# Spreading GpSimd's weight sums and splits over three blocks of a feature group in a two-layer attention and SwiGLU kernel

## The chip, the cores and the metric

The kernel runs on one core of one Trainium2 chip. A core has five engines that run side by side and wait for each other through semaphores: TensorE (PE in the profile; PEld is its weight load), VectorE (DVE), ScalarE (ACT), GpSimd (POOL) and SyncE (SP), which here issues nearly all DMAs. Each engine works through its own list of instructions in order. The metric is the device time of one execution in microseconds (us); lower is better. A time is given as the median of several runs.

## The reference

Four layers in a row on x of 2048 rows and 448 columns, all in float32: attention, feed-forward, attention, feed-forward, with the same attention weights and the same feed-forward weights both times.

```python
x = x + A(layernorm(x)); x = x + B(layernorm(x)); x = x + A(layernorm(x)); x = x + B(layernorm(x))
# A: 16 heads of 28 columns for q, one shared head for k and v
scores = einsum("bhqd,bkd->bhqk", q, k) * 28 ** -0.5;  p = softmax(scores)
o = einsum("bhqk,bkd->bhqd", p, v);  A = o @ wo
# B: gate and up 448 -> 1792, down 1792 -> 448
B = (silu(x @ w_gate) * (x @ w_up)) @ w_down
```

## The kernel before

Matrix products run in fp32r, a rounded float32. To keep precision, each operand is split in a high part (rounded to fp32r) and a low part (what is left), and a product is the sum of three matmuls. `split` does this on GpSimd with two instructions: `tensor_scalar` for the high part (L139) and `tensor_tensor` with a subtraction for the low part (L140).

The change is in the feed-forward stage, which the kernel runs twice (layers 0 and 1; in the profiled execution from about 562 to 943 us and from about 1562 to 2005 us). The 2048 rows are held as four chunks of 512. The 1792 features are 14 blocks of 128, numbered `fc`; two of them make a feature group, so there are seven groups, numbered `gi`.

Groups 0 and 6 are "old" groups. They go by `unit(gi, c, n)`: one chunk, one feature block, with gate, up and down computed straight. Groups 1 to 5 are "mixed" groups and go by `blocked(gi)`: four blocks j0 to j3, each for a pair of chunks (p = 0 or 1) and one of the group's two features A and B, in the order (0, A), (0, B), (1, A), (1, B). There, on the first two 128-row slices of the contraction, seven products take the place of eight. This needs sums and differences of weights (the tiles S, made by `sums` on GpSimd: four `tensor_tensor` of 128 columns at L800 to L803, then one split of 512 columns) and of inputs (the tiles T, made by `mix` at L787 to L792: 18 instructions for a pair of chunks; the pair p = 0 on GpSimd into the tiles `keys`, the pair p = 1 on VectorE into the tiles `mixed`).

The weights of a feature come in by `columns` (gate and up: four DMAs into the tile `wr`, two of them of 192 KB and two of 64 KB) and `loaded` (the same and a DMA of 224 KB into `wdr`). There is one buffer of `wr` and one of `wdr`, so a load waits until the readers of the one before are done. `parted` then splits them in six pieces (four of `wgh`/`wgl`, two of `wdh`/`wdl`), 12 GpSimd instructions. Three sets of split weights are kept.

The order of work is written out by hand. In a mixed block it is the string `ORDER`: names in order of issue, where a trailing "-" means the step of the block before and "--" of the one before that. The marks w1, w2, x2, x3 in it are places where `run` slips in further jobs. A step such as `Ec2`/`Ep2` first has ScalarE copy a finished down product out of a PSUM bank into a `stage` buffer (L879; there are two) and then GpSimd add it to the residual `xres` (L886). `between` (L344) is a tiny ScalarE copy from a bank that keeps two halves of TensorE work in order; TensorE waits for it. In the units the same takes are L995 (ScalarE), L996 (GpSimd) and L992 (VectorE, the other half of the adds).

At the stage's begin `rest` issues, in this order on GpSimd: the two instructions of the layer norm of chunk 3 (`rstd`, L237 and L238), the sums of feature 2, and the first six of the 18 mix steps. The other twelve follow four at a time, one lot in each of the next three units (`self.more`). VectorE's 18 mix steps (`self.extra`) begin in the unit of chunk 3: six in each of two units, then three in each of the blocks j0 and j1 of group 1, at x2 and x3. `turned` on chunk 3 transposes its normalized rows on TensorE (L287) after four small GpSimd copies (L248).

In the mixed groups GpSimd's weight work before the change is: at w1 of j0 the split of the second feature of the group; at w1 of j1 the sums and the whole split of the next group's first feature; at w1 of j3 the sums of the next group's second feature.

Of the kernel before, what the change touches and what calls it, by code (L numbers as in the profile page):

```python
# [17 lines left out]
D = 448  # L18
# [8 lines left out]
FG = 2  # L27
# [25 lines left out]
def forward(  # L53
# [72 lines left out]
    def rows3(dst, src):  # L126
        n = src.shape[1]
        nc.sync.dma_start(dst[:, 0:3], src[0:384, :].rearrange("(k p) n -> p k n", p=P))
        nc.sync.dma_start(dst[:, 3], src[384:448, :][None].to_broadcast([2, 64, n]))
# [8 lines left out]
    def split(hi, lo, raw):  # L138
        nc.gpsimd.tensor_scalar(hi, raw, 1.0, 0.0, ALU.mult, ALU.add)  # L139
        nc.gpsimd.tensor_tensor(lo, raw, hi, ALU.subtract)  # L140
# [16 lines left out]
    def columns(fc):  # L157
        fs = slice(P * fc, P * fc + P)
        r = wpool.tile([P, 4, 2, P], F32, name="wr")
        for b, src in enumerate((w_gate, w_up)):  # L160
            rows3(r[:, :, b, :], src[:, fs])
        return r

    def loaded(fc):
        r = columns(fc)
        rd = wpool.tile([P, D], F32, name="wdr")
        nc.sync.dma_start(rd, w_down[P * fc : P * fc + P, :])
        return r, rd

    def weights(fc):  # L170
        return parted(*loaded(fc))

    def parted(r, rd):
        h = wpool.tile([P, 4, 2, P], F32R, name="wgh", bufs=FG + 1)
        l = wpool.tile([P, 4, 2, P], F32R, name="wgl", bufs=FG + 1)
        dh = wpool.tile([P, D], F32R, name="wdh", bufs=FG + 1)
        dl = wpool.tile([P, D], F32R, name="wdl", bufs=FG + 1)
        for k in range(4):
            split(h[:, k], l[:, k], r[:, k])
        for ns in (slice(0, 224), slice(224, D)):  # L180
            split(dh[:, ns], dl[:, ns], rd[:, ns])
        return h, l, dh, dl

    def load_wqkv(pool, first):

# [162 lines left out]
    class Attention:  # L348
# [106 lines left out]
        def fetch(self, ms):  # L455

            r = wpool.tile([P, 2, 512], F32R, tag="wgl", name="wrq", bufs=FG + 1).bitcast(F32)
            two = wpool.tile([P, 2, 512], F32R, tag="wgh", name="q2", bufs=FG + 1)
            for z, m in enumerate(ms):
                nc.sync.dma_start(r[0:112, z, :], self.qd[0][112 * m : 112 * m + 112, :])  # L460
                self.hi[m] = two[0:112, z, :]
            nc.gpsimd.tensor_copy(two[0:112], r[0:112])
# [309 lines left out]
    class FeedForward:  # L772
# [22 lines left out]
        def sums(self, fc, r):  # L795

            raw = self.apart
            m = [raw[:, P * i : P * i + P] for i in range(4)]
            tt = nc.gpsimd.tensor_tensor
            tt(m[0], r[:, 0, 1, :], r[:, 1, 1, :], ALU.add)  # L800
            tt(m[2], r[:, 0, 0, :], r[:, 0, 1, :], ALU.subtract)
            tt(m[1], m[0], r[:, 0, 0, :], ALU.subtract)
            tt(m[3], r[:, 1, 0, :], m[1], ALU.subtract)  # L803
            split(*self.S[fc % 3], raw)
# [106 lines left out]
        def blocked(self, gi):  # L911

            A, B = groups[gi]
            if not self.blocks:
                one, two, *adds = self.pend
                self.pend = []
                self.blocks.append({"E1": one, "E2": two, "Ea0": adds[0], "Ec2": lambda: [f() for f in adds[1:]]})
                self.tmp = pers.tile([P, 4, 512], F32, name="xn")
            last = gi == mixed[-1]

            def fetch(fc):
                self.raw = loaded(fc)

            def part(fc):
                self.W[fc] = parted(*self.raw)

            def sums(fc):
                if fc // FG in mixed:
                    self.sums(fc, self.raw[0])

            jobs = [
                {"w1": [lambda: part(B)] if gi > mixed[0] else [], "w2": [lambda: fetch(A + 2)]},
                {"w1": [lambda: sums(A + 2), lambda: part(A + 2)], "w2": [lambda: fetch(A + 3)]},
                {},
                {"w1": [lambda: sums(A + 3)]},
            ]
            for j, (p, fc) in enumerate((p, fc) for p in range(2) for fc in (A, B)):
                for n, k in (("x2", 1), ("x3", 2)):
                    jobs[j][n] = [self.extra.pop(0) for _ in range(min(k, len(self.extra)))]
                self.blocks.append(self.block(p, fc))  # L940
                self.run(jobs[j])
            if last:
                o = self.blocks[-1]
                self.blocks.append({})
                ends = [[o.pop(e + k) for k in e_.split()] for e, e_ in (("E", "1 2 a0 a1 a2 a3"), ("F", "1 2 a0 a1 a2 a3"))]
                fences = [o.pop("fE"), o.pop("fF")]
                for k in ("Ec2", "Ec3", "Ep2", "Ep3"):
                    del o[k]
                self.run({})
                part(A + 3)  # L950
                self.pend, self.late = (
                    [lambda f=f, g=g: (f[0](), g()), f[1], f[2], lambda f=f: [f_() for f_ in f[3:]]] for f, g in zip(ends, fences)
                )
# [97 lines left out]
        def unit(self, gi, c, n):  # L1051
            fs = groups[gi]
            fc = fs[n]
# [50 lines left out]
            self.pend = self.down(fs, fc, d, hh, hl)  # L1104
            if n == len(fs) - 1:
                self.pend += self.accumulate(gi, c, d)
            for fs_, k in ((self.more, 4), (self.extra, 6)):
                for _ in range(min(k, len(fs_))):
                    fs_.pop(0)()
            if c == NC - 1 and mixed and not fc:  # L1110

                def load():
                    r, rd = loaded(FG + 1)
                    self.sums(FG + 1, r)
                    self.W[FG + 1] = parted(r, rd)

                self.pend.append(load)
            elif c == NC - 1 and not mixed and fc + FG + 1 < NF:
                self.pend.append(lambda: self.W.__setitem__(fc + FG + 1, weights(fc + FG + 1)))

# [41 lines left out]
        def rest(self, xb):  # L1162
# [15 lines left out]
                f()  # L1178
            self.soon.append([1, lambda: [f() for f in third[5:]]])
            if mixed:  # L1180
                self.sums(FG, columns(FG))
                self.more = self.mix(0, nc.gpsimd, self.apart, lambda o, i: nc.gpsimd.tensor_scalar(o, i, 1.0, 0.0, ALU.mult, ALU.add))
                for f in self.more[:6]:
                    f()
                del self.more[:6]
# [64 lines left out]
    for c in range(1, NC):  # L1250
        fs, got = norm_steps(c)
        n = 4 * c - 4
# [38 lines left out]
```

## Time and profile before

| | |
|---|---|
| time, median of 3 runs | 2005.31 us (2001.29 to 2008.09) |
| profiled execution, own time | 2007.16 us |
| its span, first to last instruction | 2005.4 us |
| mean granted TensorE clock | 0.992 |
| busy: TensorE / VectorE / ScalarE / GpSimd | 98% / 53% / 68% / 40% |

A row of the timeline gives the start in us from the span's start, the duration in us, the engine, the line of the kernel, the operation, the tiles written and read ("out<-in"), shapes, how many instructions were merged into the row (x), and in brackets the engine's idle time just before and what ended it. A row of the windows gives the stretch, its length, the busy time of each engine with the number of instructions, the granted TensorE clock (1.00 is full speed), the DMA engines' busy share and the GB/s. A row of the waits gives in total us, how often, and the longest.

### The profile page before, as it was taken

The page shows a single profiled execution, that of the slowest core. Times are in us where ns is not written, and L with a number is a line of the kernel's source. Part 1 is how long each engine was busy: PE and PEld are TensorE (multiplying, and loading weights), DVE is VectorE, ACT ScalarE, POOL GpSimd, SP SyncE. Part 2 cuts the span into 40 slices and gives each one's busy share as a digit, 9 for nine tenths or more (in the row PEclk, how much of TensorE's full clock was granted, in tenths as well). Part 3 has the DMA queues.
Part 4 walks back from the last instruction along what each step waited for, and adds up shares of the span by engine and source line. Part 5 has one row for each costly group of instructions (what it writes and reads, how often), then busy time and mean ns, then how long its engine had stood idle before and what let it go on. Part 6 is the DMA issues. An engine that isn't in the chain of part 4 may idle for free. (4 is left out here: it accounts for less than half of the span.)

```text
span 2005.4 us, 45589 instructions
## 1 busy us (share of the span) xinstructions
PE 1965.1 (98%) x18267; PEld 1334.2 (67%) x18267; DVE 1067.9 (53%) x1777; ACT 1357.2 (68%) x2409; POOL 803.7 (40%) x1024
## 2 busy tenths in 40 slices
PE   9999999999998999999999999999999989999998
PEld 7544545445467999999884444454454779999997
DVE  7444543545436666665654335445454467666653
ACT  4899898998953444444349989989989334444432
POOL 4212211133219667765341221212241285767740
PEclk9999999999999999999999999999999999999999
DMA  5111110211110111000131011102111100111102
GB/s 164 52 29 30 30 46 12 54 35 47 52 28 17 30 32 32 21 28 26 51 106 37 27 30 31 43 13 61 48 49 34 37 16 16 32 32 31 30 3 75
DMA packets 95511, 78.63 MB, mean 39 GB/s; under 512 B 23582, under 2 KB 78494, under 8 KB 95294
## 3 DMA queue, kind: packets, MB, share of 16 engines
q1 hardware_dynamic: 95006, 75.21, 13.3%
q8 instruction: 144, 2.36, 0.5%
q14 instruction: 73, 0.60, 0.1%
q10 hardware_dynamic: 288, 0.46, 0.1%
HBM read 56.11 MB, written 18.74 MB: 37 GB/s over the span
## 5 line engine op out<-in xcount | busy, mean ns | idle before, releaser
L661 PE MATMUL bank<-pt,vsb 128*32 128x512 f32 x4096 | 493.3, 598 | 0.3
L620 PE MATMUL bank<-qstack,keys 32*128 32x512 f32 x1536 | 484.7, 425 | 0.0
L620 PE MATMUL three<-qstack,keys 32*128 32x512 f32 x4608 | 460.3, 425 | 1.5 <-DVE vt L554 1.2
L620 PEld LDWEIGHTS three<-qstack,keys 32*128 32x128 f32 x4608 | 254.1, 182 | 295.3 <-ACT pt L633 181.1
L627 ACT ACTIVATE pt<-three 128x1536 f32<-128x1536 f32 x256 | 372.3, 1454 | 0.8 <-PE bank L661 0.5
L633 ACT ACTIVATE pt<-three 128x1536 f32<-128x1536 f32 x256 | 372.1, 1453 | 0.0
L337 PE MATMUL bank<-xh,wgh 64*128 64x512 f32 x1248 | 359.4, 395 | 5.3 <-ACT sg L860 3.9
L337 PE MATMUL bank<-wdh,h 64*128 64x448 f32 x1776 | 344.3, 368 | 1.6 <-DVE xres L884 0.9
L629 DVE COPY raw<-bank 128x512 f32<-128x512 f32 x256 | 177.6, 694 | 226.4 <-PE bank L620 223.6
L337 PE MATMUL bank<-xh,wgl 64*128 64x512 f32 x924 | 283.3, 393 | 0.0
L671 DVE TENSOR_TENSOR o<-bank,o 128x512 f32<-128x512 f32 x224 | 155.0, 692 | 240.7 <-PE bank L661 236.0
L344 ACT COPY seen<-bank 128x1 f32<-128x1 f32 x820 | 105.1, 162 | 252.1 <-PE bank L337 178.4
L700 POOL TENSOR_TENSOR o<-o 128x512 f32<-128x512 f32 x32 | 41.2, 1286 | 583.9 <-DMA o<-rd 529.0
L661 PEld LDWEIGHTS bank<-pt,vsb 128*32 128x32 f32 x4096 | 107.1, 109 | 249.8 <-issue 152.6
L337 PEld LDWEIGHTS bank<-wdh,h 64*128 64x128 f32 x1776 | 261.0, 187 | 12.6 <-DVE xres L884 2.5
L886 POOL TENSOR_TENSOR xres<-stage,xres 128x448 f32<-128x448 f32 x152 | 190.2, 1267 | 177.0 <-ACT stage L879 177.0
L337 PE MATMUL bank<-xl,wgh 64*128 64x512 f32 x816 | 247.1, 394 | 0.0
L620 PEld LDWEIGHTS bank<-qstack,keys 32*128 32x128 f32 x1536 | 243.3, 183 | 0.8 <-DVE o L671 0.6
L337 PE MATMUL bank<-wdl,h 64*128 64x448 f32 x888 | 229.5, 371 | 0.0
L851 DVE TENSOR_TENSOR xn<-bank,xn 128x512 f32<-128x512 f32 x240 | 158.0, 686 | 131.9 <-PE bank L337 85.9
L337 PEld LDWEIGHTS bank<-xh,wgh 64*128 64x128 f32 x1248 | 201.6, 186 | 15.8 <-issue 3.5
L632 ACT ACTIVATE pt<-bank 128x512 f32<-128x512 f32 x256 | 151.5, 592 | 59.7 <-PE bank L620 59.6
(200 smaller groups left out, 3243.2 us busy)
## 6 DMA issues: line engine op xcount, KB each, us to landing
o<-rd SPq DMA_DIRECT2D x32, 256.0 KB
qraw<-qd SPq DMA_DIRECT2D x128, 56.0 KB
qd<-stage SPq DMA_DIRECT2D x30, 224.0 KB
xt<-xn SPq DMA_DIRECT2D x28, 224.0 KB
wdr<-in_B_w_down_dram SPq DMA_DIRECT2D x28, 224.0 KB
wr<-in_B_w_gate_dram SPq DMA_DIRECT2D x30, 192.0 KB
wr<-in_B_w_up_dram SPq DMA_DIRECT2D x30, 192.0 KB
xn<-xt SPq DMA_DIRECT2D x7, 768.0 KB
```

Of the source, the lines that this page charges most:

```text
L337: nc.tensor.matmul(po, a, b, start=start, stop=stop, skip_group_check=True)
L344: nc.scalar.copy(seen[:, i : i + 1], po[:, 0:1])
L620: nc.tensor.matmul(three[:, j, :] if j < 3 else one, k[js, kp, ks], q[js, part, :], start=(z == 0), stop=(z == 2), tile_position=(32 * j, 0),)
L627: nc.scalar.activation(pt, three, AF.Exp, scale=SCALE)
L629: nc.vector.tensor_copy(raw, one)
L632: nc.scalar.activation(pt1, one, AF.Exp, scale=SCALE)
L633: nc.scalar.activation(pt, three, AF.Exp, scale=SCALE)
L661: nc.tensor.matmul(po[32 * j : 32 * j + 32, :], vsb[:, n % NT, :], pts[n][j], start=(n == 2 * d), stop=(n > 2 * d), skip_group_check=True,)
L671: nc.vector.tensor_tensor(acc, in_turn(po), acc, ALU.add)
L700: nc.gpsimd.tensor_tensor(rb, oraw, rb, ALU.mult)
L851: plus = lambda out, po, r: tt(by_tile(out), in_turn(po), by_tile(r), ALU.add)
L886: nc.gpsimd.tensor_tensor(r, h[e, t], r, ALU.add)
```

## The change

There are four edits.

- In the mixed groups the split of the next group's first feature (12 instructions at w1 of j1) is cut in two: three of the six pieces at w2 of j1 and the other three at w1 of j2. The sums stay at w1 of j1. The load of the feature after that moves from w2 of j1 to w2 of j2, and its sums from w1 of j3 to w2 of j3.
- At the stage's begin the sums of features 2 and 3 are both made in `rest`, ahead of the mix steps. For feature 3 this is a `columns` load of its own, four more DMAs in each layer, 512 KB. The job that made the sums of feature 3 at the end of group 0 now only loads and splits that feature's weights.
- VectorE's mix steps in the two last units of group 0 are four in each instead of six.
- In the first two mixed blocks they are two at x2 and three at x3 instead of one and two.

```diff
     def weights(fc):
-        return parted(*loaded(fc))
+        tiles, steps = parted(*loaded(fc))
+        for f in steps:
+            f()
+        return tiles
...
-        for k in range(4):
-            split(h[:, k], l[:, k], r[:, k])
-        for ns in (slice(0, 224), slice(224, D)):
-            split(dh[:, ns], dl[:, ns], rd[:, ns])
-        return h, l, dh, dl
+        steps = [lambda k=k: split(h[:, k], l[:, k], r[:, k]) for k in range(4)]
+        steps += [lambda ns=ns: split(dh[:, ns], dl[:, ns], rd[:, ns]) for ns in (slice(0, 224), slice(224, D))]
+        return (h, l, dh, dl), steps
...
-            def part(fc):
-                self.W[fc] = parted(*self.raw)
+            def part(fc, z=None):
+                if not z:
+                    self.W[fc], self.steps = parted(*self.raw)
+                for f in self.steps[3:] if z else self.steps[: 6 if z is None else 3]:
+                    f()
...
                 {"w1": [lambda: part(B)] if gi > mixed[0] else [], "w2": [lambda: fetch(A + 2)]},
-                {"w1": [lambda: sums(A + 2), lambda: part(A + 2)], "w2": [lambda: fetch(A + 3)]},
-                {},
-                {"w1": [lambda: sums(A + 3)]},
+                {"w1": [lambda: sums(A + 2)], "w2": [lambda: part(A + 2, 0)]},
+                {"w1": [lambda: part(A + 2, 1)], "w2": [lambda: fetch(A + 3)]},
+                {"w2": [lambda: sums(A + 3)]},
             ]
             for j, (p, fc) in enumerate((p, fc) for p in range(2) for fc in (A, B)):
-                for n, k in (("x2", 1), ("x3", 2)):
+                for n, k in (("x2", 2), ("x3", 3)):
...
-            for fs_, k in ((self.more, 4), (self.extra, 6)):
+            for fs_, k in ((self.more, 4), (self.extra, 4)):
...
             if c == NC - 1 and mixed and not fc:
-
-                def load():
-                    r, rd = loaded(FG + 1)
-                    self.sums(FG + 1, r)
-                    self.W[FG + 1] = parted(r, rd)
-
-                self.pend.append(load)
+                self.pend.append(lambda: self.W.__setitem__(FG + 1, weights(FG + 1)))
...
             if mixed:
-                self.sums(FG, columns(FG))
+                for fc in (FG, FG + 1):
+                    self.sums(fc, columns(fc))
```

## The prediction

> **What bounds the kernel now.** I read the page's head and chain first, then TensorE's waits, then the timeline around each wait, then windows for the granted clock.
>
> ```profile
> span 2005.4 us, 45589 instructions
> PE 43%; POOL 3%; DVE 1%; ACT 1%; issue 1%; POOLq 0%; ACTq 0%; DVEq 0%
> ```
>
> ```profile
> PE bank L337 <- ACT seen L344: 12.5, 8, 2.6
> PE bank L337 <- DVE xn L851: 8.1, 3, 4.1
> ```
>
> TensorE sets the time, and the chain leaves it only for short stretches, above all on GpSimd (3%). Only there can this change win or lose anything. The largest wait of TensorE is for ScalarE's `seen` copies in mixed blocks: 12.5 us in 8 waits, six of about 2 us. The first and the last of the six:
>
> ```profile
> 736.22 0.51 PE L337 MATMUL bank<-mixed,qstack 64*128 64x512 f32 x1 [1.92 <-ACT seen L344]
> ...
> 1850.40 0.49 PE L337 MATMUL bank<-mixed,kdiag 64*128 64x512 f32 x1 [2.62 <-ACT seen L344]
> ```
>
> All six stand at the end of block j1 in groups 2, 3 and 4 of both layers. One of them, engine by engine:
>
> ```profile
> 1715.87 0.46 POOL L800 TENSOR_TENSOR apart<-wr 128x128 f32<-128x128 f32 x1
> 1720.08 0.42 POOL L139 TENSOR_SCALAR wgh<-wr 128x256 fp32r<-128x256 f32 x1
> ...
> 1728.02 4.47 POOL L886 TENSOR_TENSOR xres<-stage,xres 128x448 f32<-128x448 f32 x4
> ```
>
> ```profile
> 1718.90 1.15 ACT L879 COPY stage<-bank 128x448 f32<-128x448 f32 x2 [0.47 <-PE bank L337]
> ...
> 1729.20 0.53 ACT L879 COPY stage<-bank 128x448 f32<-128x448 f32 x1 [3.26 <-POOL xres L886]
> ```
>
> ```profile
> 1729.84 0.79 PE L337 MATMUL bank<-mixed,qstack 64*128 64x512 f32 x1 [1.93 <-ACT seen L344]
> ```
>
> GpSimd runs the sums (4.2 us, 1715.87 to 1720.08) and the whole split (7.9 us, to 1728.02) in one go. Behind them wait the two adds of the E step, whose stage buffers ScalarE filled from 1718.90. ScalarE's next take needs one of these buffers, idles 3.26 us, and its `seen` copies stand behind it, so TensorE idles 1.93 us. The wait then costs a second time:
>
> ```profile
> 1684.00:1698.00 14.00, 14.00 (x129) 13.85 (x127) 10.10 (x15) 6.85 (x26) 8.53 (x10) 1.00 0.00 1
> ...
> 1726.20:1743.20 17.00, 15.07 (x121) 14.63 (x120) 8.31 (x14) 6.26 (x25) 8.49 (x9) 0.90 0.16 46
> 1743.20:1758.00 14.80, 14.80 (x137) 14.70 (x136) 9.90 (x16) 7.58 (x27) 9.07 (x10) 1.00 0.00 1
> ```
>
> ```profile
> 736.60:740.00 3.40, 3.40 (x19) 3.35 (x18) 1.33 (x3) 1.70 (x4) 2.24 (x3) 0.50 0.08 25
> ...
> 1791.30:1794.70 3.40, 3.40 (x21) 3.40 (x19) 2.58 (x4) 1.18 (x6) 1.09 (x1) 0.50 0.02 6
> ```
>
> An undisturbed block takes 14.0 us; the two after the wait take 17.0 and 14.8, 3.8 us too long for an idle of 1.93. The rest is the clock: in 3.4 us after the wait it is 0.50. That is so after four of the six waits (the rows are the first and the last of the four); each such stretch loses half of itself, 1.7 us.
>
> **The change part by part.** *Cutting the split.* After the change GpSimd does in j1 the sums, then the E adds, then half a split, and the other half in j2. In the rows above the E adds would start at 1720.1 instead of 1728.0, and four adds took 4.47, so two are done at about 1722.4; half a split follows until about 1726.3, just when the F take comes; its add is late by less than 1 us and nothing waits for it. The other half at w1 of j2 holds up E adds by at most 4 us, as the sums now do in j1. Sums at w2 instead of w1 of j3 come behind the E adds and hold up none of them; their result is read a group later, and nothing else is queued before the next F take. I count nothing for them, 1 us if that cover is short. The moved load (five DMAs, issued a block later on SyncE, with nothing queued behind it there) has a block of 14 us until the sums read it. So all six waits go. Idle about 12.1 us (12.5 less two short waits), clock 4 x 1.7 = 6.8, and about 0.2 us each that the 3.8 us shows above 1.93 + 1.7: 20 us gained. Lower end 12, if only the idle comes back.
>
> *Sums of feature 3 at the stage's begin.* This is what speaks against the change. The rows in order, layer 1, then two other loads into the same tile `wr`:
>
> ```profile
> 1593.28 0.46 POOL L800 TENSOR_TENSOR apart<-wr 128x128 f32<-128x128 f32 x1
> ...
> 1595.14 0.46 POOL L803 TENSOR_TENSOR apart<-wr,apart 128x128 f32<-128x128 f32 x1
> ...
> 1597.77 1.28 POOL L787 TENSOR_TENSOR apart<-xh 128x512 f32<-128x512 f32 x1
> ...
> 1605.57 2.58 POOL L996 TENSOR_TENSOR xres<-stage,xres 128x448 f32<-128x448 f32 x2
> ...
> 1613.11 0.76 POOL L248 COPY xn<-xn 128x64 f32<-128x64 f32 x4
> ```
>
> ```profile
> 1595.63 0.37 SPq L128 DMA_DIRECT2D wr<-in_B_w_gate_dram  x1
> ```
>
> ```profile
> 1608.29 0.96 ACT L995 COPY stage<-bank 128x448 f32<-128x448 f32 x2
> ```
>
> ```profile
> 1613.40 0.85 PE L287 MATMUL bank<-ident,xn 128*128 128x128 f32 x4 [0.45 <-POOL xn L248]
> ```
>
> ```profile
> 957.39 0.38 SPq L128 DMA_DIRECT2D wr<-in_A_wq_dram  x1
> ```
>
> ```profile
> 963.04 0.94 POOL L139 TENSOR_SCALAR wh<-wr 128x896 fp32r<-128x896 f32 x1 [5.51 <-DMA wr<-in_A_wq_dram]
> ```
>
> ```profile
> 146.42 1.65 SPq L594 DMA_DIRECT2D wr<-in_A_wo_dram  x4
> ...
> 150.33 0.94 POOL L139 TENSOR_SCALAR woh<-wr 128x896 fp32r<-128x896 f32 x1 [3.94 <-DMA wr<-in_A_wo_dram]
> ```
>
> From 1593 to 1613 GpSimd has no idle time, and at its end TensorE already waits for it (0.45 us for the copies L248). Whatever is put into this list ahead of L248 goes onto the path one to one. Put in: the second sums, 4.5 us as the first (1593.28 to 1597.77), and ahead of them a wait for the new load. With one `wr`, its DMAs can start only when the first sums have read it: the next load is issued at 1595.63, right behind L803. From such an issue to GpSimd's first use went 5.65 us (957.39 to 963.04) and 3.9 us (146.42 to 150.33); I take 4.7, between them. So the sums start at 1600.3, not at 1597.77, and everything behind moves by 2.5 + 4.5 = 7.0 us (6.3 to 8.2 by the two ends). ScalarE's L995 at 1608.29 also needs the adds L996, then at about 1612.6, and TensorE loses most of the 7 us there and the rest at L248. Two layers: 14 us. For the clock, with such long idle, none to one half-speed stretch more that is not waited out anyway in each layer: 0 to 1.7, I take 0.5. Together 15 us lost (12.6 to 20).
>
> *VectorE's mix steps and the removed sums at the end of group 0.*
>
> ```profile
> 1631.83 0.60 ACT L1088 ACTIVATE sg<-bank 128x512 f32<-128x512 f32 x1 [2.15 <-PE bank L337]
> ```
>
> ```profile
> 1633.52 0.68 DVE L1089 TENSOR_TENSOR sg<-bank,sg 128x512 f32<-128x512 f32 x1
> ...
> 1640.46 1.10 DVE L790 TENSOR_TENSOR qraw<-qraw,xl 128x512 f32<-128x512 f32 x1
> 1641.48 2.07 DVE L851 TENSOR_TENSOR xn<-bank,xn 128x512 f32<-128x512 f32 x3
> ...
> 1664.84 1.54 DVE L792 TENSOR_TENSOR mixed<-qraw,mixed 128x512 fp32r<-128x512 f32 x1
> 1666.33 1.29 DVE L851 TENSOR_TENSOR xn<-bank,xn 128x512 f32<-128x512 f32 x2
> ```
>
> ```profile
> 1642.21 0.79 PE L337 MATMUL bank<-xh,kdiag 64*128 64x512 f32 x1 [3.39 <-DVE xn L851]
> ...
> 1654.58 0.59 PE L337 MATMUL bank<-xh,wgh 64*128 64x512 f32 x1 [2.10 <-ACT sg L860]
> ```
>
> ```profile
> 1641.10:1648.00 6.90, 5.79 (x28) 5.04 (x30) 4.34 (x8) 0.80 (x3) 4.25 (x7) 0.51 0.36 106
> ```
>
> L851 of j0 is late because VectorE does six mix steps in each of the two units before it. Two fewer in the first unit let L1089 begin 1.1 us earlier, when ScalarE's silu is done (1632.43); two fewer in the second, at some 0.9 us (1.10 for L790), save 1.8. L851 comes about 2.9 us earlier; TensorE, which also waited for L1089, is 1.1 earlier at this place, and its 3.39 us of idle shrink to about 1.6. The half-speed stretch behind it (clock 0.51 over 6.9 us, 3.4 lost) shrinks by one half or goes. Against it, j0 and j1 each get two steps more, about 1.9 us. In j1 a mix step already ran right up to the combining L851 at 1666.33, with no idle between; in j0 VectorE waits for TensorE in between. I put 1.5 us of both on the path. With the half-speed stretch that may follow the wait before j1 in its new place, I count 1.7 of the clock's 3.4, and that gives 2.9 + 1.7 - 1.5 = 3.1. TensorE's wait of 2.10 before j1 stays. Net 3 us per layer, 6 for both, between 1 and 10 (half of L851's gain with all four steps on the path, or all of it with none). GpSimd's sums that went from here (5 us) save nothing: their cover was idle time before the next L996.
>
> Sum: 20 + 6 - 15 = 11 us, less 1 for small delays of VectorE beside GpSimd's work now in three blocks instead of one. The profiled execution took 2007.16 us, so 1997; it is 1.9 us above the median of the runs, which would go to 1995. I say 1996.
>
> **Rivals.** (1) *The begin of the stage eats the gain.* Load wait by the longer row (8.2 us shift per layer), one half-speed stretch each (1.7), and only 2 us from VectorE: 20 + 2 - 1 - 20 = +1, time about 2005. For it: the path has no slack at all there; against it: it needs every end at once. The shift per layer would have to reach 12.5 us before the other 25 us (20 + 6 - 1) are gone.
>
> (2) *The waits of j1 stay.* If the F take is held up by the half split now in front of its add, as it was by the adds behind the whole split, the idle moves from one block end to the next, and only the loss at the begin remains: 2005 + 15 - 6 = 2014. It decides from the point at which the second E add ends after the F take, 1725.9; I have it end at 1722.4, 3.5 us earlier. If both halves together hold back more than that, at least half of the 20 us stays.
>
> (3) *The added load costs nothing*, because TensorE's holes at the begin are made up in waits that stand behind them (3.39 and 2.10 us): 2005 - 25 = 1980. Against it: those waits hang on VectorE and ScalarE, which move along with TensorE.
>
> (4) A gate that halves the clock only after a whole idle stretch: then the 1.9 us waits cost only their idle, 12 us, and the 5 us holes at the begin would each earn a half-speed stretch: 12 + 4 - 18 = -2, time 2007. The rows exclude it here: 0.50 after 1.92 us.
> The Trainium skill states this rule in "TensorE: Matmul & The Clock Gate", Part 1 and the table of "Why this matters for your kernels" (cold after one idle window of about 3.4 us, so avoid gaps above 3 us). This trace agrees on the stretch's length and differs on how much idle it takes.
>
> **How the numbers follow.** Forecast 0.58 (1986 to 2002), rival 1 0.21, rival 2 0.14, rival 3 0.06, rival 4 0.01. A measurement of this kernel tells about 0.3%, 6 us. Faster than that: most of the forecast (0.51) and rival 3, 0.57. Within: the rest of the forecast and rivals 1 and 4, 0.29. Slower: rival 2, 0.14. The range leaves out rivals 2 and 3: 1986 to 2008, its low end from the upper ends of the VectorE term and of the 20 us.
>
> **What would show it.** Right: no `seen` wait of 2 us in groups 2 to 4, all blocks at 14.0 us, GpSimd's adds between sums and half split; in each layer's begin a GpSimd wait for `wr` of 1.5 to 3.5 us and a TensorE hole of some 5 us at L995 and L248; L851's wait below 2 us. Wrong: a new wait for L886 at the begin of j2, a hole at the begin much longer than 8 us, or C12 of j1 late enough to stall j2.

## The result, and the profile after

The changed kernel takes 2001.11 us (median of 20 executions, 1998.94 to 2004.07), the kernel before 2005.40 (20 executions, 2001.14 to 2008.09). The ratio is 0.9983, with a 95% interval of 0.9976 to 0.9989: 4.3 us faster, where 9.4 were forecast (1996); that is less than the 0.3% that the prediction set as the least that can be told from no change. The profiled execution took 2000.67 us, with a span of 1998.9.

The lines of the changed kernel are numbered a little higher: L337 is L338, L344 is L345, L851 is L852, L860 is L861, L886 is L887, L995 is L999, L996 is L1000, L248 is L249, L800 is L801, L1089 is L1093.

TensorE's waits after the change:

```profile
PE bank L338 <- ACT stage L999: 7.8, 2, 4.0
PE bank L338 <- ACT sg L861: 6.6, 4, 3.1
PE bank L338 <- DVE xn L852: 4.3, 4, 2.2
PE bank L288 <- POOL xn L249: 3.4, 2, 1.7
...
PE bank L338 <- ACT seen L345: 0.4, 2, 0.2
```

The `seen` waits went from 12.5 us to 0.4, and a new first line stands at the stage's begin. GpSimd in block j1 of group 2, layer 1:

```profile
1722.75 1.30 POOL L140 TENSOR_TENSOR qstack<-apart,qstack 128x512 fp32r<-128x512 f32 x1
1724.00 2.30 POOL L887 TENSOR_TENSOR xres<-stage,xres 128x448 f32<-128x448 f32 x2
1726.26 0.42 POOL L139 TENSOR_SCALAR wgh<-wr 128x256 fp32r<-128x256 f32 x1
...
1729.48 1.06 POOL L140 TENSOR_TENSOR wgl<-wr,wgh 128x256 fp32r<-128x256 f32 x1
1730.56 1.17 POOL L887 TENSOR_TENSOR xres<-stage,xres 128x448 f32<-128x448 f32 x1
```

The E adds now stand between the sums and the half split (1724.00), and the F add follows the half split without holding up anyone. GpSimd at the begin of layer 1's stage, and TensorE beside it:

```profile
1591.88 0.46 POOL L801 TENSOR_TENSOR apart<-wr 128x128 f32<-128x128 f32 x1
...
1599.72 0.81 POOL L801 TENSOR_TENSOR apart<-wr 128x128 f32<-128x128 f32 x1 [3.42 <-DMA wr<-in_B_w_up_dram]
...
1604.42 1.29 POOL L788 TENSOR_TENSOR apart<-xh 128x512 f32<-128x512 f32 x1
...
1612.14 2.22 POOL L1000 TENSOR_TENSOR xres<-stage,xres 128x448 f32<-128x448 f32 x2
...
1618.95 0.76 POOL L249 COPY xn<-xn 128x64 f32<-128x64 f32 x4
```

```profile
1613.89 0.74 PE L338 MATMUL bank<-wdh,h 64*128 64x448 f32 x1 [3.96 <-ACT stage L999]
...
1619.24 1.12 PE L288 MATMUL bank<-ident,xn 128*128 128x128 f32 x4 [1.70 <-POOL xn L249]
```

GpSimd waits 3.42 us for the second load. From the first sums to the copies L249 it now takes 27.07 us (1591.88 to 1618.95), before the change 19.83 (1593.28 to 1613.11): 7.2 us more. Around the two holes of TensorE the clock is low, in both layers:

```profile
623.00:633.20 10.20, 8.22 (x35) 5.92 (x37) 2.67 (x4) 4.06 (x13) 9.70 (x13) 0.50 0.01 2
1612.90:1623.10 10.20, 7.51 (x33) 5.38 (x35) 2.68 (x4) 4.37 (x13) 9.70 (x14) 0.50 0.01 2
```

**Where the time went.** ScalarE's copy L853 (L852 before) stands once in each mixed block, so its starts cut the stage into lengths. The first three in layer 1:

```profile
1643.08 0.59 ACT L853 COPY xn<-bank 128x512 f32<-128x512 f32 x1 [0.36 <-PE bank L338]
1661.36 0.59 ACT L853 COPY xn<-bank 128x512 f32<-128x512 f32 x1 [0.50 <-PE bank L338]
1676.35 0.59 ACT L853 COPY xn<-bank 128x512 f32<-128x512 f32 x1
```

From the first sums (1591.88) to j0 it takes 51.20 us, from j0 to j1 18.28, from j1 to j2 14.99. The table has these lengths for the kernels that the text goes by, layer 0 / layer 1, from their profiled executions; the kernels below the second are those of the experiments.

| kernel | first sums to j0 | j0 to j1 | j1 to j2 | j2 to the last block |
|---|---|---|---|---|
| before | 42.83 / 43.43 | 21.16 / 21.82 | 14.04 / 14.03 | 248.33 / 249.17 |
| after | 50.98 / 51.20 | 18.92 / 18.28 | 14.98 / 14.99 | 239.88 / 239.50 |
| jobs_alone | 42.86 / 43.47 | 20.41 / 19.83 | 14.04 / 14.04 | 239.91 / 239.59 |
| undo_begin | 41.92 / 42.39 | 21.24 / 19.04 | 15.02 / 15.17 | 239.69 / 239.38 |
| undo_again | 41.93 / 42.40 | 21.18 / 16.34 | 14.98 / 14.96 | 239.51 / 239.20 |
| begin_alone | 52.08 / 52.84 | 19.78 / 16.84 | 14.04 / 14.26 | 246.93 / 249.39 |
| filled_more | 49.36 / 49.79 | 19.58 / 18.58 | 14.98 / 14.97 | 239.70 / 239.30 |
| sooner | 42.08 / 42.65 | 16.52 / 17.21 | 14.03 / 14.01 | 239.49 / 239.16 |

Before against after, both layers together: 15.9 us lost ahead of j0, 5.8 gained from j0 to j1, 1.9 lost from j1 to j2, 18.1 gained in the rest. In the kernels of the table with the cut split the last column agrees within 0.5 us in each layer. The column j0 to j1 moves by up to 5 us between kernels that have the same code there, and even between undo_begin and undo_again, which are one kernel run twice.

### The profile page after: what moved, and what is told of

Its sections match the earlier page's. It is cut to its first block, busy times and chain, and to the rows that moved or that the text cites. A ratio compares the mean times of both kernels' runs of the same rounds, so it can differ in the third digit from the quotient of the medians.

```text
span 1998.9 us, 45604 instructions
## 1 busy us (share of the span) xinstructions
PE 1962.7 (98%) x18267; PEld 1324.4 (66%) x18267; DVE 1069.5 (54%) x1777; ACT 1355.7 (68%) x2409; POOL 798.9 (40%) x1024
## 5 line engine op out<-in xcount | busy, mean ns | idle before, releaser
L338 PE MATMUL bank<-xh,wgh 64*128 64x512 f32 x1248 | 357.4, 396 | 7.0 <-ACT sg L861 6.6
L338 PE MATMUL bank<-wdh,h 64*128 64x448 f32 x1776 | 341.3, 366 | 9.4 <-ACT stage L999 7.8
L338 PE MATMUL bank<-xh,wgl 64*128 64x512 f32 x924 | 281.5, 393 | 0.0
L345 ACT COPY seen<-bank 128x1 f32<-128x1 f32 x820 | 105.1, 163 | 247.7 <-PE bank L338 174.2
L338 PEld LDWEIGHTS bank<-wdh,h 64*128 64x128 f32 x1776 | 255.9, 185 | 21.3 <-ACT stage L999 8.6
L887 POOL TENSOR_TENSOR xres<-stage,xres 128x448 f32<-128x448 f32 x152 | 187.0, 1242 | 163.1 <-ACT stage L880 162.9
L338 PE MATMUL bank<-xl,wgh 64*128 64x512 f32 x816 | 245.3, 394 | 0.0
L338 PE MATMUL bank<-wdl,h 64*128 64x448 f32 x888 | 226.4, 370 | 0.0
L852 DVE TENSOR_TENSOR xn<-bank,xn 128x512 f32<-128x512 f32 x240 | 157.8, 685 | 104.1 <-PE bank L338 84.2
L338 PEld LDWEIGHTS bank<-xh,wgh 64*128 64x128 f32 x1248 | 199.1, 186 | 19.9 <-POOL qstack L140 6.6
```

The source lines that it names most:

```text
L338: nc.tensor.matmul(po, a, b, start=start, stop=stop, skip_group_check=True)
L345: nc.scalar.copy(seen[:, i : i + 1], po[:, 0:1])
L852: plus = lambda out, po, r: tt(by_tile(out), in_turn(po), by_tile(r), ALU.add)
L887: nc.gpsimd.tensor_tensor(r, h[e, t], r, ALU.add)
```

## The experiments

Each result stands beside executions of the kernel before on the same chip, whose medians were 2003.2 to 2004.6. jobs_alone to undo_begin ran together, then jobs_again to own_tile, then sums_later, filled, j3_w1 and sooner, then filled_more and best. The changed kernel ran only with the result, where before stood at 2005.40. A difference to the changed kernel is therefore also given with each of the two held against the before that ran beside it; the two ways differ by 1.7 to 2.2 us, and neither is the surer one.

**One part at a time.** jobs_alone is the kernel before with the cut split and the moved jobs only (`weights`, `parted` and `part` are cut in steps as in the change, which isn't shown again):

```diff
-                {"w1": [lambda: sums(A + 2), lambda: part(A + 2)], "w2": [lambda: fetch(A + 3)]},
-                {},
-                {"w1": [lambda: sums(A + 3)]},
+                {"w1": [lambda: sums(A + 2)], "w2": [lambda: part(A + 2, 0)]},
+                {"w1": [lambda: part(A + 2, 1)], "w2": [lambda: fetch(A + 3)]},
+                {"w2": [lambda: sums(A + 3)]},
```

> The kernel before with one edit: the split of a feature group's weights is cut in two and spread over three blocks, with the sums; everything else as before. Forecast's term: six waits of about 2 us and their four half-speed stretches go, 20 us, so 1985. From the two traces: the stretch from j2 of the first mixed group to the last block is 18.1 us shorter after the change, so 1987. Rival (the waits of j1 only move to the begin of j2): no gain or a few us, 2000 to 2005. In its trace the first theory wants no seen wait of about 2 us, the rival wants them at another block.

Measured: 1986.45 us, ratio 0.9907 (0.9892 to 0.9922), 18.1 us gained. The forecast's 20 holds nearly, and the waits didn't move to another block.

begin_alone is the kernel before with only this:

```diff
-                    self.sums(FG + 1, r)
...
-                self.sums(FG, columns(FG))
+                for fc in (FG, FG + 1):
+                    self.sums(fc, columns(fc))
```

> The kernel before with one edit: the sums of feature 3 stand at the stage's begin, with a load of their own, and no longer in the load at the end of group 0. Forecast's term: 15 us lost, so 2020 (2018 to 2025). By the two traces (15.9 us longer from the first sums to j0, and VectorE's edit gave back about 2 us of that): 18 us lost, so 2023. Rival, the added work finds room in waits behind it: 2005 to 2010.

Measured: 2018.57 us, ratio 1.0078 (1.0064 to 1.0092), 14.0 us lost. Its way from the first sums to j0 is 9.3 and 9.4 us longer than before (table), but j0 to j1 came out 1.4 and 5.0 us shorter.

vector_alone is the kernel before with only this:

```diff
-                for n, k in (("x2", 1), ("x3", 2)):
+                for n, k in (("x2", 2), ("x3", 3)):
...
-            for fs_, k in ((self.more, 4), (self.extra, 6)):
+            for fs_, k in ((self.more, 4), (self.extra, 4)):
```

> The kernel before with one edit: VectorE's mix steps, four and not six in the two units before the first block, and one more at each of x2 and x3 of j0 and j1. Forecast's term: 6 us gained, so 1999 (between 1995 and 2004). By the two traces also about 6 us. Rival: the gain in front of j0 comes back whole in j0 and j1, so 2005.

Measured: 1998.84 us (1995.44 to 2003.73, 10 executions), ratio 0.9973 (0.9963 to 0.9983), 5.7 us gained, as forecast.

undo_begin is the changed kernel with begin_alone's edit taken back:

```diff
-                self.pend.append(lambda: self.W.__setitem__(FG + 1, weights(FG + 1)))
+                def load():
+                    r, rd = loaded(FG + 1)
+                    self.sums(FG + 1, r)
+                    self.W[FG + 1], steps = parted(r, rd)
+                    for f in steps:
+                        f()
+
+                self.pend.append(load)
...
-                for fc in (FG, FG + 1):
-                    self.sums(fc, columns(fc))
+                self.sums(FG, columns(FG))
```

> The changed kernel with one part undone: the sums of feature 3 are back in the load at the end of group 0; the cut split and VectorE's steps stay. If the begin costs what the forecast put on it (15 us), 1986; if what the two traces show (18 us), 1983; if the begin costs little and the other two parts simply gave less than forecast (7 us and not 26), about 1998.

Measured: 1987.02 us, ratio 0.9908 (0.9892 to 0.9923). By its time alone this is the first branch, 1986. But the parts don't add up: cut split and VectorE's edit gain 18.1 and 5.7 alone, and 17.5 together. Beside the cut split VectorE's edit seemed worth nothing.

**Is VectorE's gain lost, or hidden by chance?** Both kernels ran once more.

> The kernel of the run jobs_alone once more, for more executions beside the next one. Four executions gave 1986.5. If VectorE's edit is worth its 6 us beside the cut split too and those four fell on favourable places of the clock's 3.4-us stretches, this comes out at 1987 to 1989 and undo_again at 1982 to 1984. If VectorE's edit is worth nothing beside the cut split, both stay at 1986 to 1987.

> The kernel of the run undo_begin (cut split and VectorE's steps) once more. Its trace against that of jobs_alone: TensorE waits 4.8 us less in all, but 3 more half-speed stretches of 3.4 us. If the stretches were chance, 1982 to 1984 and 3 to 5 us under jobs_again; if they belong to the kernel, 1986 to 1987, no difference.

Measured: jobs_again 1985.18, undo_again 1982.41. Over the eight executions of each the medians are 1985.7 and 1983.8: by these VectorE's edit gains 1.9 us beside the cut split. But the executions of the second kernel spread from 1981.45 to 1987.68, and by resampling the executions the gain lies anywhere between -1.9 and 3.9 us. The next run has it beside both other parts:

```diff
-                for n, k in (("x2", 2), ("x3", 3)):
+                for n, k in (("x2", 1), ("x3", 2)):
...
-            for fs_, k in ((self.more, 4), (self.extra, 4)):
+            for fs_, k in ((self.more, 4), (self.extra, 6)):
```

> The changed kernel with VectorE's mix steps as before (six in the two units, one and two at x2 and x3); cut split and sums at the begin stay. By the forecast's term VectorE's edit is worth 6 us: 2007. If that edit is worth nothing beside the cut split: 2001. If terms simply add by the runs of single parts (1986.5 + 14): 2000.5.

Measured: 2004.15 us (11 executions), so 3.0 us above the changed kernel (4.8 by the before beside each). The edit's three values are thus 5.7, 1.9 and 3.0. By the same resampling the first lies between 2.1 and 7.7 and the last between 0 and 5.1, so the three overlap, and their differences are not shown by the times. The traces show two things that move them; the first is the clock. TensorE's waits at j0 in jobs_again, and windows over the idle time of the two longest and the work behind them:

```profile
649.85 0.50 PE L338 MATMUL bank<-xh,kdiag 64*128 64x512 f32 x1 [4.07 <-DVE xn L852]
...
1632.75 0.50 PE L338 MATMUL bank<-xh,kdiag 64*128 64x512 f32 x1 [3.38 <-DVE xn L852]
```

```profile
647.20:654.00 6.80, 4.15 (x24) 3.69 (x26) 4.87 (x9) 0.41 (x2) 5.09 (x8) 0.75 0.21 62
1630.30:1637.10 6.80, 4.35 (x26) 3.84 (x28) 5.01 (x8) 0.69 (x2) 4.89 (x8) 0.75 0.28 74
```

The same in undo_again:

```profile
646.77 0.79 PE L338 MATMUL bank<-xh,kdiag 64*128 64x512 f32 x1 [2.75 <-DVE xn L852]
...
1630.25 0.49 PE L338 MATMUL bank<-xh,kdiag 64*128 64x512 f32 x1 [2.08 <-DVE xn L852]
```

```profile
645.90:652.70 6.80, 5.93 (x30) 5.15 (x32) 5.08 (x9) 0.94 (x3) 5.57 (x9) 0.50 0.26 70
...
1627.70:1634.50 6.80, 4.72 (x43) 3.79 (x41) 6.59 (x10) 1.69 (x8) 6.38 (x10) 1.00 0.15 39
```

VectorE's edit shortens the wait for L852 by 1.3 us in each layer. But the longer wait of 4.07 us was followed by one half-speed stretch of 3.4 us (0.75 over two), the shorter one of 2.75 by two (0.50), and one of 2.08 by none. The half-speed stretches don't follow the length of a wait alone. They begin on a grid of 3.41 us, and it matters how the wait lies on it. In the trace of before a wait of 3.39 us had two half-speed stretches behind it (0.51 over 6.9 us); the same wait, 3.38, had one here.

The second is a wait that VectorE's edit makes longer, the one before j1. VectorE in j0 of layer 1 and TensorE's wait behind it, in no_vector:

```profile
1658.97 1.29 DVE L852 TENSOR_TENSOR xn<-bank,xn 128x512 f32<-128x512 f32 x2 [0.28 <-PE bank L338]
```

```profile
1662.35 0.46 PE L338 MATMUL bank<-xh,wgh 64*128 64x512 f32 x1 [1.68 <-ACT sg L861]
```

and in the changed kernel, with two mix steps more in j0:

```profile
1650.42 1.54 DVE L791 TENSOR_TENSOR qraw<-qraw,xl 128x512 f32<-128x512 f32 x1
1652.00 1.28 DVE L792 CAST mixed<-qraw 128x512 fp32r<-128x512 f32 x1
...
1653.73 1.27 DVE L852 TENSOR_TENSOR xn<-bank,xn 128x512 f32<-128x512 f32 x2
```

```profile
1654.44 0.63 ACT L860 ACTIVATE xn<-xn 128x512 f32<-128x512 f32 x1 [2.48 <-DVE xn L852]
```

```profile
1657.52 0.76 PE L338 MATMUL bank<-xh,wgh 64*128 64x512 f32 x1 [3.05 <-ACT sg L861]
```

VectorE's idle time in front of this L852 was 1.28 and 0.28 us in no_vector (0.63 and 1.10 in before); the changed kernel has none there, because the added steps stand right in front of it. ScalarE waits for L852 with L860, its `sg` (L861) comes later, and TensorE waits for that. In layer 0 the wait went from 1.86 to 2.78 us. In the eight traces without the added steps in j0 it is 1.68 to 2.10 us; in the eight with them it is above 2.0 in 13 cases of 16, and 3.0 or more in nine.

**What in the begin costs.** own_tile loads what the second sums read ahead of the first sums, into the tile `qraw`, which is idle there. The diff is against the changed kernel:

```diff
-                for fc in (FG, FG + 1):
-                    self.sums(fc, columns(fc))
+                r3 = qraw.rearrange("p (k b n) -> p k b n", k=2, b=2)
+                for b, src in enumerate((w_gate, w_up)):
+                    nc.sync.dma_start(r3[:, :, b, :], src[0:256, P * (FG + 1) : P * (FG + 2)].rearrange("(k p) n -> p k n", p=P))
+                self.sums(FG, columns(FG))
+                self.sums(FG + 1, r3)
```

> The changed kernel, where the second load at the stage's begin goes to a tile of its own (two of the four row parts, which is all that the sums read) and is issued ahead of the first sums, so that GpSimd doesn't wait 3.1 to 3.4 us for it; the 4.5 us of sums stay. The forecast's shift of 7.0 us per layer was 2.5 of load wait and 4.5 of sums. If the shift goes onto the end one to one: 6.5 us less than the changed kernel, 1994.5. If the wait is covered and only the sums' work or the clock costs: 2001. If the load costs more than its wait (the half-speed stretches behind the 4-us hole go with it): 1988 to 1991.

Measured: 1994.67 us (6 executions), ratio to before 0.9961 (0.9947 to 0.9975): 6.4 us less than the changed kernel (4.7 by the before beside each). GpSimd in layer 1:

```profile
1590.43 1.30 POOL L140 TENSOR_TENSOR sums<-apart,kdiag 128x512 fp32r<-128x512 f32 x1
1591.81 0.46 POOL L801 TENSOR_TENSOR apart<-qraw 128x128 f32<-128x128 f32 x1
...
1610.96 0.75 POOL L249 COPY xn<-xn 128x64 f32<-128x64 f32 x4
```

The second sums follow the first with no wait. From the first sums to j0 it takes 47.04 and 47.97 us, 3.9 and 3.2 less than in the changed kernel, so GpSimd's wait of 3.1 to 3.4 us per layer comes off one to one there.

sums_later has load and sums behind the copies L249. Its sums write the tile `apart` while a mix step keeps an intermediate there, so one of the mixed inputs comes out changed; the instructions are the same in number and size.

```diff
-            self.soon.append([1, lambda: [f() for f in third[5:]]])
+            self.soon.append([1, lambda: [f() for f in third[5:]] + [self.sums(FG + 1, columns(FG + 1)) for _ in mixed[:1]]])
...
-                for fc in (FG, FG + 1):
-                    self.sums(fc, columns(fc))
+                self.sums(FG, columns(FG))
```

> The changed kernel, where the sums of feature 3 with their load stand in GpSimd's list right behind the four copies L249 that TensorE waits for, and not in front of them. Work and load are the same. If what the begin costs is the place in the list (nothing behind GpSimd's list has slack until those copies, and idle time of 2.7 to 3.2 us stands behind them): 14 to 17 us less than the changed kernel, 1984 to 1987. If it is the work and the load as such: 2000. If the adds L1000 of the next unit become late in turn: 1990 to 1995.

Measured: 1986.89 us, ratio 0.9921 (0.9907 to 0.9934), 14.2 us under the changed kernel (12.0 by the before beside each). GpSimd and TensorE in layer 1:

```profile
1604.99 0.76 POOL L249 COPY xn<-xn 128x64 f32<-128x64 f32 x4
1605.71 0.45 POOL L801 TENSOR_TENSOR apart<-wr 128x128 f32<-128x128 f32 x1
```

```profile
1605.28 0.85 PE L288 MATMUL bank<-ident,xn 128*128 128x128 f32 x4 [0.45 <-POOL xn L249]
```

TensorE's wait for the copies is 0.45 us again, as before the change. So most of the cost is the place in the list and not the work. The work isn't quite free behind the copies either: the time is 3.1 us above undo_begin's 1983.8, and from L249 to j0 it takes 23.45 and 24.00 us, in undo_begin 22.09 and 22.56.

**What the clock costs there.** filled and filled_more add matmuls in the unit with the holes; nothing reads their results.

```diff
+                if mixed and (gi, c, n) == (0, 2, 1):
+                    side_by_side(
+                        [(pg[0], o, *e) for o, e in zip(lists[0], ends[0])],
+                        [(pg[1], o, *e) for o, e in zip(lists[3], ends[0])],
+                    )
                 side_by_side(
...
                 first.pop(0)()
+                if mixed and (gi, c, n) == (0, 2, 1):
+                    spare = [bank(LOW)[1] for _ in range(2)]
+                    side_by_side(
+                        [(spare[0], o, i == 0, i == 10) for i, o in enumerate(lists[0])],
+                        [(spare[1], o, i == 0, i == 10) for i, o in enumerate(lists[3])],
+                    )
                 for f in mid[1:]:
```

> The changed kernel with matmuls added on TensorE at the begin, whose result nothing uses: 22 ahead of the first half of the unit with the holes, 22 behind its down products, some 2.6 us each, so that the holes of 3.9 and 1.7 us are mostly filled and the clock stays up. GpSimd's list, and with it the time of the copies L249, isn't touched. The forecast put 0.5 us per layer on the clock there. If the three half-speed stretches per layer (10.2 us) cost half of themselves: 10 us less, 1991. If only what stands behind the copies counts, since the rest lies beside the wait: about 1.7 per layer, 1997.5. If the clock costs nothing there: 2001 or, with matmuls that come out too long, 2003.

Measured: 2001.22 us, no gain. The way from the first sums to j0 was 49.47 us in layer 0, without a half-speed stretch, and 52.90 in layer 1, where 1.7 us of idle time stayed in one stretch and two half-speed stretches followed. filled_more has 30 added matmuls in the first place and 18 in the second:

```diff
-                    side_by_side(
-                        [(pg[0], o, *e) for o, e in zip(lists[0], ends[0])],
-                        [(pg[1], o, *e) for o, e in zip(lists[3], ends[0])],
-                    )
+                    for k in (4, 11):
+                        side_by_side(
+                            [(pg[0], o, *e) for o, e in zip(lists[0][:k], ends[0])],
+                            [(pg[1], o, *e) for o, e in zip(lists[3][:k], ends[0])],
+                        )
...
-                        [(spare[0], o, i == 0, i == 10) for i, o in enumerate(lists[0])],
-                        [(spare[1], o, i == 0, i == 10) for i, o in enumerate(lists[3])],
+                        [(spare[0], o, i == 0, i == 8) for i, o in enumerate(lists[0][:9])],
+                        [(spare[1], o, i == 0, i == 8) for i, o in enumerate(lists[3][:9])],
```

> The run filled once more with the added matmuls in other lengths (30 ahead of the first half, 18 behind the down products), so that in both layers less than 1.5 us stay idle in any 3.4-us window. In layer 0 of filled no half-speed stretch stood there and the way from the first sums to j0 took 49.5 us, against 51.0 in the changed kernel and 41.9 without the sums at the begin. If the clock is worth that 1.5 us in each layer, both layers show 49.5 to 49.9 and the time is about 3 us under the changed kernel, 1998. If the 9 us of the begin are all GpSimd's list: 2001, with 51 in both layers. If the clock costs the whole 5 us per layer: 1991.

Measured: 1998.61 us (11 executions), ratio 0.9978 (0.9969 to 0.9987), 2.5 us under the changed kernel (0.8 by the before beside each, so the time alone doesn't settle it). Windows over the holes' place in both layers:

```profile
612.00:632.00 20.00, 18.70 (x152) 14.62 (x150) 5.13 (x8) 5.38 (x16) 19.10 (x20) 1.00 0.13 39
1602.00:1622.00 20.00, 18.70 (x151) 14.73 (x149) 5.12 (x8) 5.50 (x16) 19.10 (x20) 1.00 0.14 40
```

With the clock at 1.00 throughout, the way to j0 takes 49.36 and 49.79 us instead of 50.98 and 51.20, though the copies L249 come 27.06 and 27.07 us after the first sums, as in the changed kernel (26.94 and 27.07). So the clock costs 1.5 us per layer up to j0, if the added matmuls cost nothing themselves; j0 to j1 is 0.7 and 0.3 us longer, so not all of it reaches the end. Of the 5.1 us that 10.2 us at half speed lose, the rest lies beside the wait for GpSimd's copies, which end when they end.

**Two remedies.** j3_w1 is jobs_alone with the sums of j3 at w1 again, as before the change:

```diff
-                {"w2": [lambda: sums(A + 3)]},
+                {"w1": [lambda: sums(A + 3)]},
```

> The kernel of jobs_alone with one step as before: the sums of the fourth block (j3) at w1 and not at w2. In the traces with w2 the four blocks from j3 to j0 take 14.2 to 14.5 us instead of 14.0, about 2 us in all, with a wait of TensorE for VectorE's L852. If the sums' place does that: 14.0 again and 2 us less than jobs_alone (1985.2 to 1986.5), so 1984. If it comes from the split spread over three blocks: no change.

Measured: 1984.20 us, 1.5 under the 1985.7 of jobs_alone's eight executions, about as much as the executions scatter. The traces are clearer: all four blocks from j3 to j0 take 13.99 to 14.00 us in each layer. In jobs_alone these had 14.22 to 14.53. There, VectorE beside the sums at w2, and TensorE:

```profile
1686.31 1.73 DVE L871 TENSOR_TENSOR h<-xn,h 128x512 fp32r<-128x512 f32 x1 [0.69 <-ACT h L867]
```

```profile
1688.69 0.97 PE L338 MATMUL bank<-keys,qstack 64*128 64x512 f32 x6 [0.25 <-DVE xn L852]
```

Beside GpSimd's sums L871 takes 1.71 to 1.73 us in three of these eight blocks and 1.02 in the other five; the three are the blocks that are 0.5 us longer, the five those that are 0.2 longer. In the other blocks behind group 1 it takes 0.68 to 0.95. L852 behind the row shown is late by 0.25.

sooner is undo_begin with VectorE's mix steps begun one unit earlier, in units (0,2,1), (0,3,0) and (0,3,1):

```diff
-                for n, k in (("x2", 2), ("x3", 3)):
+                for n, k in (("x2", 1), ("x3", 2)):
...
-                        if mixed and (gi, c, n) == (0, 3, 0):
+                        if mixed and (gi, c, n) == (0, 2, 1):
```

> The kernel of undo_begin (cut split, sums of feature 3 at the end of group 0), where VectorE's mix steps begin one unit earlier: four in each of three units instead of two, and one and two again at x2 and x3 of j0 and j1. In the traces with VectorE's edit j1 to j2 takes 15.0 us and not 14.04, and TensorE waits 2.1 to 2.8 us for L852 at j0. If the mix steps in front of L852 and in j0 and j1 are the cause, the 1 us per layer of j1 to j2 goes (2 us) and 1980 to 1983 comes out, against 1982.4 to 1987.0 of undo_begin. Rival: VectorE's flips of the third unit before j0 are then late, 1987 to 1990.

Measured: 1977.87 us (1976.57 to 1978.60), ratio 0.9876 (0.9861 to 0.9891). TensorE's waits at j0, and the same place by windows:

```profile
647.04 0.49 PE L338 MATMUL bank<-xh,kdiag 64*128 64x512 f32 x1 [2.40 <-DVE xn L852]
656.45 0.47 PE L338 MATMUL bank<-xh,wgh 64*128 64x512 f32 x1 [1.71 <-ACT sg L861]
...
1625.07 0.57 PE L338 MATMUL bank<-xh,kdiag 64*128 64x512 f32 x1 [1.70 <-DVE xn L852]
1636.01 0.47 PE L338 MATMUL bank<-xh,wgh 64*128 64x512 f32 x1 [1.70 <-ACT sg L861]
```

```profile
1620.00:1640.00 20.00, 16.60 (x130) 14.15 (x130) 15.72 (x21) 6.79 (x25) 16.58 (x21) 0.91 0.14 39
640.00:660.00 20.00, 15.89 (x135) 13.39 (x133) 15.50 (x22) 7.00 (x25) 18.57 (x24) 1.00 0.14 39
```

j1 to j2 is back at 14.0 us, and all but one of the half-speed stretches at j0 and j1 are gone: 6 us under undo_begin's 1983.8, and 2 below the 1980 to 1983 expected. The wait before j1 is 1.7 us again, as in the other kernels without the added steps in j0.

best is sooner with the edit of j3_w1 added.

> The kernel of the run sooner with the sums of j3 at w1 again, as in j3_w1: what the single runs found, together. sooner gave 1977.9; the blocks from j3 to j0 at 14.0 and not 14.2 to 14.5 take 2 us off: 1976. If the two share their gain: 1978.

Measured: 1977.00 us (1973.22 to 1980.10), ratio 0.9862 (0.9845 to 0.9878). It beats both kernels, by 27 us (2003.7 beside it) and 24; what j3's place adds to sooner can't be told apart (0.9 us).

## Why the prediction was wrong

The direction was right, and so was what was said of the cut split and of GpSimd's list at the begin. The step that failed is VectorE's term, and beside it the clock's loss was mis-sized at the begin. Put in one after the other, the parts gained 18.4 (2004.1, the mean of the two medians of before beside these runs, to 1985.7), gained 1.9 (to 1983.8) and lost 17.3 (to 2001.1). The prediction had 20, 6 and 15, and 1 for small delays. The measured parts come to 3.0, and the result's own comparison gave 4.3. How the miss divides depends on the order: with the begin put in second it lost 19.0 (jobs_again to no_vector, which ran together) and VectorE's steps gained 3.0 behind it.

- *Cutting the split, 20 us.* All six waits went, and the idle time didn't move to another block's end. The clock's 4 x 1.7 was one execution's count: in the traces of before, begin_alone and vector_alone together, 10 of the 18 such waits had a half-speed stretch behind them (four, three and three), which makes 5.7 us for six and not 6.8. Of the cover "I count nothing for them, 1 us if that cover is short", the sums at w2 of j3 were the exception: 0.2 to 0.5 us in each of eight blocks, through VectorE's L871. Moving them back returned 1.5 by the medians.
- *VectorE's steps, 6 us: the step that failed.* The working was 2.9 + 1.7 - 1.5 per layer. The first unit's 1.1 us came (first sums to j0 is 0.9 to 1.1 shorter, jobs_alone against undo_begin). L852's wait shrank by 1.3, not 1.8. Two parts were wrong. First, "TensorE's wait of 2.10 before j1 stays" did not hold. The price of the added steps was put at 1.5 because "in j0 VectorE waits for TensorE in between", but in front of the combining L852 that idle time was only 0.3 to 1.3 us, and the wait before j1 grew by 0.9 and 1.4 us (no_vector to the changed kernel, one trace each). j1 to j2 grew by 0.9 and 1.0, so the price was 1.8 and 2.3. Second, the 1.7 for the half-speed stretch behind L852's wait, which "shrinks by one half or goes", was no fixed gain: the two stretches in the one trace of before were one place on the grid among many. In jobs_alone, which has the same waits, one stretch followed each of them, and in undo_begin the shorter waits had no fewer behind them. The same edit measured 5.7, 1.9 and 3.0 us in three surroundings, with wide intervals; how much of the missing gain is the one part and how much the other, these runs don't settle.
- *The sums at the begin, 15 us.* GpSimd's wait was 3.13 and 3.42 us, inside the 1.5 to 3.5 named; the list shifted by 7.2 us at L249 (forecast 7.0) and own_tile and sums_later confirm both of its parts. The clock was put at 0.5 per layer and is about 1.5 (filled_more): two holes slowed three stretches, and the one behind L249 isn't waited out. Twice 7.2 + 1.5 is 17.4. Measured were 17.3 (16.0 by the before beside each kernel), 19.0 without VectorE's edit, and 14.0 alone; how much of these differences is the grid's chance and how much is made up behind j0, these runs don't settle.
- *The rivals.* Rival 1 (2005) was the nearer account of the begin: some 1.5 us of clock per layer and a small gain from VectorE (2 there, 1.9 and 3.0 measured) both came out, only the shift stayed at 7.2 and not 8.2. (The 8.2 was itself a slip: a load of 5.65 us makes a wait of 3.5, and with 4.5 of sums 8.0.) 2001 lies between it and the forecast. Rival 2 (waits of j1 stay) is out by jobs_alone, rival 3 (the begin free) by sums_later and begin_alone.
- *Rival 4*, a gate that needs a whole idle stretch, is out by more than the one row. I laid the 3.41-us grid over the matmul records of all 16 traces, in the feed-forward stages. Rounded to tenths, a stretch at full speed with 1.0 to 1.6 us of idle time was followed by a half-speed one in 2 cases of about 50, with 1.7 or 1.8 us in 10 of about 20, with 1.9 or more in every one of about 45. So a wait of 2.0 us slows the clock only if nearly all of it falls into one stretch: about (3.4 + 2.0 - 2 x 1.75) / 3.4, over half of all places, which fits the four of six in before and the 10 of 18 above. The Trainium skill, "TensorE: Matmul & The Clock Gate", Part 1, asks for a whole idle window of about 3.4 us. The traces agree on 3.4 us and show about half of it idle to be enough.

## What to carry over

Price a wait of TensorE by its idle time first, and add the clock's loss as a mean over places on the grid, not as the one profile happened to show it; an edit that only shortens a wait may leave the stretch behind it. On an in-order engine whose list has no slack up to a point that others wait for, put new work behind that point, and give its load a buffer of its own. When work is moved into a gap of an engine, look how long the gap is and who waits behind it: VectorE's added steps met idle time of 0.3 to 1.3 us, and what didn't fit came out in TensorE's next wait. An edit that is worth a few us should be run in more than one surrounding and with enough executions, since the same edit here measured 1.9 to 5.7 us with intervals as wide as that.

## What was not expected of the hardware

A stretch that already runs at half speed is kept there by much less idle time: of 18 such stretches with 0.5 us or more of it, 17 were followed by another at half speed, while at full speed up to 1.6 us was mostly harmless (the 2 cases of about 50 above). This is how holes of 3.96 and 1.70 us slowed three stretches in a row. And a slow clock is free where TensorE would wait anyway: of the 5.1 us lost at each begin, 3.6 lay beside GpSimd's list.
